# Attention, channel mix and gated convolution in one kernel: new tables for the planner that orders its steps

## The chip, the cores and the metric

The kernel runs on one core of a Trainium2 chip. The time is device time in microseconds (us). TensorE (PE) does the matmuls, VectorE (DVE), ScalarE (ACT) and GpSimd (POOL) the elementwise work; SP issues most of the transfers and POOL those that add to what is there. Every engine works through its own instructions in the order in which the program has them.

## The reference

Three layers follow each other, on 4 batches of 576 tokens of 512 values, in fp32.

```python
# attention: B=4, H=8, S=576, D=64
q_d, k_d, v_d = means of q, k, v over 4 neighbouring tokens
out_up = repeat(softmax(scale * q_d @ k_d.T) @ v_d, 4)
scores = where(abs(i - j) < 4, scale * q @ k.T, -1e9)
x = out_up + softmax(scores) @ v
# channel mix, 512 -> 1024 -> 512
xk = mu_k * x + (1 - mu_k) * x_prev
xr = mu_r * x + (1 - mu_r) * x_prev
k = relu(xk @ w_k)
x = sigmoid(xr @ w_r) * (k * k @ w_v)
# gated convolution, 512 -> 1024 -> 512
h = relu(x @ w_in)
conv_out = convolution of h along the tokens, 3 taps per channel
out = (h * sigmoid(conv_out)) @ w_out
```

## The kernel before

**Attention.** It goes by batch and group of four heads, eight groups in all. The local scores (`local_scores`, L543) put a mask into PSUM with a few bf16 matmuls (L560) and add, block by block of 32 queries, fp32 matmuls with 38 columns each (L569), in two steps of up to 40 instructions. The trace shows two passes for one such fp32 instruction of the program, so 40 instructions are 80 passes. The scores of the pooled keys and queries (`down_scores`, L618) are L634, their softmax's last step, `norm`, is L676 on ACT or L678 on DVE; L707 and L762 transpose probabilities, `down_out` multiplies by the pooled values (L730), and `local_out` by the values (L781, 32 columns, 144 passes a group); L796 adds the two into `xT`. The local matmuls are very short, and there are many of them.

**Channel mix.** fp32 is made of two fp32r parts, high and low, and each product of three matmuls: high by high, low by high, high by low. `mix` (L929) takes half a batch (288 tokens): the up projection is 8 steps of 12 matmuls of 288 columns (L939), the down projection 8 steps of 12 and 12 (L988). The first half of batch 0 is done with exact fp32 weights instead (`first_mix`, L865; L876 and L906). The relu, the square and the splitting of k lie at L958 to L976, on ACT and DVE (the high copy is L969 on ACT or L971 on DVE).

**The rest.** In six chunks of 384 tokens: `gate` (L1260, r), `hidden` (L1301, h, with the convolution on DVE and ACT) and `outp` (L1381, the output).

**Transfers.** `load` (L392) is an SP transfer; `load_sum` (L394) sums four planes of pooled input: one load by SP, and three accumulating ones through POOL's queue (L400), each of which waits for the one ahead. So `kqd` (pooled keys and queries) and `vd` are filled. There is one `kqd` buffer for the groups after the first two, which are split, and an L634 step of 20 instructions (40 passes) reads it; six L634 steps are whole in this way. `vw` holds the values for the local output, `vw_f` and `kq_f` (and `kqd_f`) those of the other group of batch 0. Weights come as 512 KB pieces into one of three `st_d` (L418), and ACT and DVE split them into their parts (L405 to L450). The first matmuls of the program are fill matmuls (L1043), which compute nothing that is used.

**The order.** Each piece of work is a `step` of class `Program` (L83): the engine, an estimated time, a function that emits the instructions, what it reads and writes, and a due time. A step that may go to two engines has two times, and the planner takes the engine. `order` (L126) plays the program through, engine by engine: of the steps that are ready it takes the one that must start earliest. Two tables shift this by the tag of a step, such as `('lo', 2, 0, 0)` for the local output of batch 2, group 0, `('up', b, half)`, `('dn', b, half)` for the projections, or `('wk', 0, column)` for a weight piece:

```python
        latest = [t - EARLY.get(k, 0.0) for t, k in zip(latest, self.tags)]   # L142
        ready = [HOLD.get(k, 0.0) for k in self.tags]                         # L145
            i = min((i for i in q if ready[i] <= at + 1e-9), key=lambda i: (latest[i], i))   # L166
```

HOLD (L25) is the earliest time, in the planner's microseconds, at which a step may stand, EARLY (L38) how much more urgent it is made. What comes out is one list of instructions for each engine.

Of the kernel before, what the change touches and what calls it, by code (L numbers as in the profile page):

```python
# [22 lines left out]


HOLD = {  # L25
    ('dn', 0, 0): 14.9, ('dn', 0, 1): 34.2, ('dn', 1, 0): 21.3, ('dn', 1, 1): 18.4, ('dn', 2, 1): 14.8,
    ('dn', 3, 0): 0.4, ('lc', 2): 18.9, ('lc', 4): 152.4, ('ld', 0, 0, 10): 22.5, ('ld', 0, 1, 0): 8,
    ('ld', 0, 1, 10): 38, ('ld', 2, 0, 0): 11.4, ('ld', 2, 1, 0): 129.6, ('ld', 3, 0, 0): 67.1,
    ('ld', 3, 1, 0): 4.1, ('mu',): 13.5, ('o', 0): 32.1, ('o', 1): 56.9, ('o', 2): 6.4, ('o', 3): 49.8,
    ('o', 5): 44.2, ('sx', 0): 98.7, ('sx', 1): 2.6, ('wi', 0, 0): 2.5, ('wi', 0, 128): 65.5,  # L30
    ('wi', 0, 256): 118.8, ('wi', 0, 384): 49.7, ('wi', 0, 512): 34.8, ('wi', 0, 640): 19.4,
    ('wi', 0, 896): 0.5, ('wk', 0, 0): 20.4, ('wk', 0, 128): 17, ('wk', 0, 256): 5.3, ('wk', 0, 512): 0.5,
    ('wk', 0, 640): 16.4, ('wk', 0, 768): 24.2, ('wk', 0, 896): 0.5, ('wo', 2, 0): 4.2, ('wo', 3, 0): 1.6,
    ('wo', 5, 0): 20.6, ('wo', 6, 0): 26.2, ('wr', 0, 384): 71, ('wv', 0, 0): 4.5, ('wv', 0, 256): 34.3,
    ('wv', 0, 384): 7.3, ('wv', 1, 0): 20.5, ('wv', 1, 128): 31.2, ('wv', 1, 384): 46.9,
}

EARLY = {  # L38
    ('dn', 0, 0): 362.8, ('dn', 0, 1): -820.5, ('dn', 1, 0): -80.4, ('dn', 1, 1): -10.7,
    ('dn', 2, 0): -11.7, ('dn', 2, 1): 29.4, ('dn', 3, 0): 13.7, ('dn', 3, 1): 108.6,  # L40
    ('do', 0, 0, 0): -7.5, ('do', 0, 0, 10): -7.4, ('do', 0, 1, 0): -7.9, ('do', 0, 1, 10): 3,
    ('do', 1, 0, 0): -35.3, ('do', 1, 1, 0): -69.4, ('do', 2, 0, 0): -57.6, ('do', 2, 1, 0): 8.8,
    ('do', 3, 0, 0): 141.6, ('do', 3, 1, 0): 81.4, ('ds', 0, 0, 0): 15.6, ('ds', 0, 0, 10): -410.1,
    ('ds', 0, 1, 0): 4.2, ('ds', 0, 1, 10): 180.9, ('ds', 1, 0, 0): 566, ('ds', 1, 1, 0): 679.3,
    ('ds', 2, 0, 0): 163.7, ('ds', 2, 1, 0): 192.7, ('ds', 3, 0, 0): 300.4, ('ds', 3, 1, 0): -16.4,
    ('fill',): -104.7, ('g', 0): 286.6, ('g', 1): 157.2, ('g', 2): -6.9, ('g', 3): -203.9, ('g', 4): -59.3,
    ('g', 5): 119.1, ('h', 0): 10.9, ('h', 1): -155.2, ('h', 2): -58.5, ('h', 3): -17, ('h', 4): 265.4,
    ('h', 5): 1.6, ('kd', 0, 0, 10): -275.5, ('kd', 0, 1, 0): -135, ('kd', 0, 1, 10): 27.6,
    ('lc', 0): -572.8, ('lc', 1): -205.6, ('lc', 2): 141.2, ('lc', 3): 35, ('lc', 4): -3.8,
    ('lc', 5): 10.4, ('ld', 0, 0, 10): 92.2, ('ld', 0, 1, 0): -2.8, ('ld', 1, 0, 0): 85.9,  # L50
    ('ld', 1, 1, 0): -94.4, ('ld', 2, 0, 0): -275.8, ('ld', 3, 0, 0): -51.1, ('lo', 0, 0, 0): 119.5,
    ('lo', 0, 0, 10): -900.4, ('lo', 0, 1, 0): 61.7, ('lo', 0, 1, 10): 80.1, ('lo', 1, 0, 0): 333,
    ('lo', 2, 0, 0): 355.4, ('lo', 2, 1, 0): 66.8, ('lo', 3, 0, 0): -108.4, ('lo', 3, 1, 0): 586.9,
    ('mp', 0, 0): -756.6, ('mp', 0, 1): -384, ('mp', 1, 0): 197.6, ('mp', 1, 1): -9.5,
    ('mp', 2, 0): -209.6, ('mp', 2, 1): -23.5, ('mp', 3, 0): -20.3, ('mp', 3, 1): -78.3, ('mu',): 73.3,
    ('o', 0): -74, ('o', 1): -220.6, ('o', 2): -203.8, ('o', 3): 416.8, ('o', 5): 6.9,
    ('s', 0, 0, 0): -72.1, ('s', 0, 0, 10): -1335, ('s', 0, 1, 0): -34.3, ('s', 0, 1, 10): -58.1,
    ('s', 1, 0, 0): 382.4, ('s', 1, 1, 0): 29.3, ('s', 2, 0, 0): -39.6, ('s', 2, 1, 0): -999.4,
    ('s', 3, 0, 0): 172.5, ('s', 3, 1, 0): 162.8, ('sx', 0): 90.9, ('sx', 1): -4.2, ('sx', 2): 271.9,
    ('sx', 3): -239.4, ('up', 0, 0): -6.3, ('up', 0, 1): 532, ('up', 1, 0): -0.5, ('up', 1, 1): 94.2,  # L60
    ('up', 2, 0): 589.6, ('up', 2, 1): -2561.6, ('up', 3, 0): 36.8, ('up', 3, 1): -64.9, ('wi', 0, 0): 142,
    ('wi', 0, 128): -81.8, ('wi', 0, 256): -26.9, ('wi', 0, 384): 29.3, ('wi', 0, 512): -117.8,
    ('wi', 0, 640): 2.1, ('wi', 0, 768): -71.3, ('wi', 0, 896): 98, ('wk', 'first'): -1373.2,
    ('wk', 'parts', 0, 0): 39.2, ('wk', 'parts', 0, 128): 105.1, ('wk', 'parts', 0, 256): -391,
    ('wk', 'parts', 0, 384): 158.6, ('wk', 'parts', 0, 512): 67.9, ('wk', 'parts', 0, 640): 32,
    ('wk', 'parts', 0, 768): -824.5, ('wk', 'parts', 0, 896): -168.4, ('wk', 0, 128): -290,
    ('wk', 0, 256): -8, ('wk', 0, 384): 15.7, ('wk', 0, 512): -49.1, ('wk', 0, 640): 166,
    ('wk', 0, 768): 19.3, ('wk', 0, 896): -54.8, ('wo', 0, 0): -27.1, ('wo', 1, 0): 177.6,
    ('wo', 2, 0): 57.8, ('wo', 3, 0): 23.3, ('wo', 4, 0): 188, ('wo', 5, 0): -343.2, ('wo', 6, 0): -6,
    ('wo', 7, 0): 29.1, ('wr', 0, 0): -224.1, ('wr', 0, 128): -173, ('wr', 0, 256): -286.5,  # L70
    ('wr', 0, 384): 265.7, ('wv', 'first'): -29.6, ('wv', 'parts', 0, 0): -23.2,
    ('wv', 'parts', 0, 128): 13.8, ('wv', 'parts', 0, 256): -424.1, ('wv', 'parts', 0, 384): 49,
    ('wv', 'parts', 1, 0): 7, ('wv', 'parts', 1, 128): 3.2, ('wv', 'parts', 1, 256): 13.4,
    ('wv', 'parts', 1, 384): -98.2, ('wv', 0, 0): 8.5, ('wv', 0, 256): -5.3, ('wv', 0, 384): 109.3,
    ('wv', 1, 0): 34.9, ('wv', 1, 128): -120.4, ('wv', 1, 256): 355.1, ('wv', 1, 384): -37.6,
}


# [7 lines left out]
class Program:  # L86
# [19 lines left out]
    def step(self, engine, us, f, r=(), w=(), due=None, slack=1.0):  # L106
        n = len(self.steps)
        deps = set()
        for k in r:
            if k in self.writer:  # L110
                deps.add(self.writer[k])
        for k in w:
            deps.update(self.readers.pop(k, ()))
            if k in self.writer:
                deps.add(self.writer[k])
        for k in r:
            self.readers.setdefault(k, set()).add(n)
        for k in w:
            self.writer[k] = n
        deps.discard(n)  # L120
        self.steps.append((engine, us, f, due, slack))
        self.tags.append(self.tag)
        self.deps.append(deps)
        return n
# [100 lines left out]
def dve(n):  # L225
    return 0.13 + 1.1e-3 * n
# [22 lines left out]
def tile_local_attention__then__channel_mix__then__conv_glu(  # L249
# [24 lines left out]
    SD = S // FAC  # L274
# [70 lines left out]
    first = tc.alloc_tile_pool(name="first", bufs=1)  # L345
# [39 lines left out]
    def ring(name, tiles, one=0):  # L385

        i = count[name] = count.get(name, -1) + 1
        i %= one or len(tiles)
        return tiles[i], (name, i)
# [68 lines left out]
    def group(b, gp):  # L458
# [3 lines left out]
        g = {"kq": ring("kq", kq_t, int(b > 0)), "kqd": ring("kqd", kqd, int(b > 0)), "vw": ring("vw", vw_t, int(b > 0)),  # L462
             "vd": ring("vd", vd_t, int(b > 0))}
# [154 lines left out]
        def down_scores(i0, i1):  # L618
            tag("ds", i0)
            q0, m, qs = down_blocks(i0, i1)  # L620
            nq = len(qs)
            pst, pk = ring("a2", a2_t)
            pd, pdk = ring("pd", pd_t, int(b > 0))
            sm, smk = ring("sums", sums)
# [48 lines left out]
            def norm(eng):  # L673
# [6 lines left out]
                    )  # L680

            step(
                ("DVE", "ACT"), (dve(nq * SD), 0.2 * nq + 0.1), norm, [(smk, "r", r) for r in range(2)],
                [(pdk, r) for r in range(2)], slack=SL[i0 > 0],
            )

# [61 lines left out]
        def local_out(i0, i1):  # L748
# [24 lines left out]
            for pr, hp in enumerate(pairs):  # L773
# [30 lines left out]
                step("DVE", 0.28 + 0.97e-3 * nt, add, [odk], [(pk, 0), (pk, 1)] + ks, slack=SL[i0 > 0])  # L804

        return {"loads": loads, "kqd": pooled_kq, "s": local_scores, "ds": down_scores,
                "do": down_out, "lo": local_out}

# [323 lines left out]
    wo = [t.rearrange("p k c -> p (k c)").rearrange("p (k c) -> p k c", c=DM) for t in wk_t]  # L1132
# [354 lines left out]
```

## Time and profile before

| | before |
|---|---|
| median of 3 runs | 579.89 us (578.99 to 582.29) |
| the profiled execution | 580.39 us |
| its span | 578.7 us |
| mean granted clock of TensorE | 0.991 |
| PE busy | 556.3 us, 96% of the span, 5960 matmul passes |
| DVE busy | 365.4 us, 63% |
| ACT busy | 339.0 us, 59% |
| POOL busy | 47.4 us, 8% |

The profiled execution is 0.50 us above the median of the runs. The share of busy time is a mean over a front part, in which attention, channel mix and all weight loads overlap, and a back part of long matmuls.

### The profile page before, as it was taken

How to read it: one execution, taken by the hardware profiler on the slowest of the kernel's cores; microseconds unless marked ns; L12 is line 12 of the kernel's file. 1: busy time of each engine (PE TensorE's matmuls, PEld its weight loads, DVE VectorE, ACT ScalarE, POOL GpSimd, SP SyncE). 2: the span in 40 equal slices, each digit the busy share in tenths (PEclk: the TensorE clock that was granted, in tenths of full speed). 3: DMA queues.
4: the chain of work that ended last, by engine and by line, in shares of the span. 5: the costliest groups of instructions: out<-in, count | busy, mean ns of one | idle time of the engine just before them, and what ended most of it. 6: DMA issues, size and time to landing. Idle time of an engine off the chain costs nothing.

```text
span 578.7 us, 14428 instructions
## 1 busy us (share of the span) xinstructions
PE 556.3 (96%) x5960; PEld 510.6 (88%) x5960; DVE 365.4 (63%) x749; ACT 339.0 (59%) x810; POOL 47.4 (8%) x150
## 2 busy tenths in 40 slices
PE   7899999969999999799999999999999999999996
PEld 4677789959999899799999989899988998998995
DVE  4898989746344551549307999389747695294580
ACT  3678888638675573559649856356435445263441
POOL 5001111020110202100000000000000000000000
PEclk9989999999999999999999999999999999999999
DMA  8479898991875856608212430401200300100101
GB/s 329 156 222 243 287 295 218 292 327 37 251 209 162 202 161 125 159 2 264 74 42 61 146 109 8 148 11 36 75 38 38 110 1 37 56 1 0 56 1 54
DMA packets 30938, 72.97 MB, mean 126 GB/s; under 512 B 3288, under 2 KB 14040, under 8 KB 29848
## 3 DMA queue, kind: packets, MB, share of 16 engines
q1 hardware_dynamic: 26552, 64.09, 33.3%
q0 software_dynamic: 4320, 7.97, 8.4%
q8 instruction: 46, 0.75, 0.5%
q14 instruction: 20, 0.16, 0.1%
HBM read 57.88 MB, written 14.16 MB: 124 GB/s over the span
## 4 chain that ended last, share of the span: by engine, by line
PE 87%; DVE 4%; issue 3%; ACT 2%; DMA 2%; POOL 1%; ACTq 0%; POOLq 0%; DVEq 0%
PE a L1381 17%; PE mm L939 16%; PE mm L988 14%; PE a L1301 8%; PE mm L1301 7%; PE mm L1260 4%; PE a L1260 4%; PE a L781 3%; PE mm L876 3%; PE mm L906 3%; PE a L730 2%; DMA xT<-x_d 2%; PE a L569 2%; PE a L707 2%; PE a L762 2%
## 5 line engine op out<-in xcount | busy, mean ns | idle before, releaser
L1381 PE MATMUL a<-wk,wv 128*128 128x512 f32 x432 | 100.4, 390 | 0.0
L939 PE MATMUL mm<-xk,wk 128*128 128x288 f32 x672 | 95.7, 302 | 3.3 <-issue 3.3
L939 PEld LDWEIGHTS mm<-xk,wk 128*128 128x128 f32 x672 | 92.5, 194 | 4.2 <-issue 4.0
L988 PE MATMUL mm<-k,wv 128*128 128x288 f32 x672 | 95.9, 298 | 0.1
L1381 PEld LDWEIGHTS a<-wk,wv 128*128 128x128 f32 x432 | 81.0, 188 | 16.2
L988 PEld LDWEIGHTS mm<-k,wv 128*128 128x128 f32 x672 | 90.2, 188 | 1.2 <-ACT k L969 0.2
L976 DVE TENSOR_TENSOR k<-tmp,k 128x288 fp32r<-128x288 f32 x56 | 25.5, 455 | 47.8 <-ACT k L969 47.5
L1301 PE MATMUL mm<-k,wi 128*128 128x386 f32 x288 | 53.0, 338 | 0.7 <-ACT k L1285 0.4
L1301 PE MATMUL a<-k,wi 128*128 128x386 f32 x288 | 52.7, 338 | 0.0
L1301 PEld LDWEIGHTS mm<-k,wi 128*128 128x128 f32 x288 | 50.7, 188 | 1.7 <-ACT k L1285 0.7
L1301 PEld LDWEIGHTS a<-k,wi 128*128 128x128 f32 x288 | 50.8, 188 | 0.2
L1346 DVE TENSOR_SCALAR tmp<-h,cw_sb 128x384 f32<-128x384 f32 x48 | 20.0, 416 | 41.5 <-ACT h L1334 22.2
L1356 ACT ACTIVATE tmp<-tmp 128x384 f32<-128x384 f32 x48 | 25.2, 525 | 27.6 <-DVE tmp L1350 27.5
L958 ACT ACTIVATE tmp<-mm 128x288 f32<-128x288 f32 x56 | 22.9, 409 | 25.4 <-PE mm L939 25.3
L1396 ACT ACTIVATE xT<-a 128x512 f32<-128x512 f32 x18 | 10.3, 595 | 40.3 <-PE a L1381 40.2
L1350 DVE SCALAR_TENSOR_TENSOR tmp<-h,cw_sb,tmp 128x384 f32<-128x384 f32 x48 | 29.7, 619 | 2.6
L1347 DVE SCALAR_TENSOR_TENSOR tmp<-h,cw_sb,tmp 128x384 f32<-128x384 f32 x48 | 29.7, 619 | 2.4
L1368 DVE TENSOR_TENSOR wv<-tmp,wv 128x384 fp32r<-128x384 f32 x48 | 25.5, 553 | 8.9 <-ACT wv L1366 8.6
L1260 PE MATMUL mm<-xk,wr 128*128 128x386 f32 x144 | 26.8, 338 | 0.4 <-ACT h L1329 0.4
L923 ACT COPY tmp<-mm 128x288 f32<-128x288 f32 x32 | 12.5, 395 | 25.0 <-PE mm L988 15.9
L796 DVE TENSOR_TENSOR xT<-a,od 128x288 f32<-128x288 f32 (+2 forms) x40 | 13.8, 392 | 20.6 <-PE a L781 20.3
L400 POOL DMA_DIRECT2D kqd<-in_kqp x18 | 16.0, 889 | 130.4 <-DMA kqd<-in_kqp 81.5
(161 smaller groups left out, 894.5 us busy)
## 6 DMA issues: line engine op xcount, KB each, us to landing
vw<-in_vw SPq DMA_DIRECT2D x7, 1152.0 KB, 8.0
kq<-in_kq SPq DMA_DIRECT2D x6, 1152.0 KB
kqd<-in_kqp POOLq DMA_DIRECT2D x18, 288.0 KB, 7.4
v_d<-tmp SPq DMA_DIRECT2D x32, 144.0 KB, 4.1
x_d<-xT SPq DMA_DIRECT2D x16, 288.0 KB, 4.9
out_dram<-xT SPq DMA_DIRECT2D x18, 256.0 KB, 2.0
st_d<-in_moe_w_k SPq DMA_DIRECT2D x8, 512.0 KB, 5.1
st_d<-in_moe_w_v SPq DMA_DIRECT2D x8, 512.0 KB, 5.2
```

The lines of the kernel that those rows point to most:

```text
L939: nc.tensor.matmul(pst[:, 0:NH], lhsT=wk_t[wt][:, kt, mt * P:(mt + 1) * P], rhs=xk[:, xs, kt, :], start=(kt == 0 and g == 0), stop=(kt == ...
L958: lambda r=r, pst=pst: nc.scalar.activation(r, pst[:, 0:NH], AF.Relu), (), [pk, rk],
L976: ("DVE",), (dve(NH),), lambda e, r=r, kh=kh, kl=kl: e.tensor_sub(kl, r, kh.bitcast(F32)),
L988: nc.tensor.matmul(pst[:, 0:NH], lhsT=wv_t[wt][:, kt, mt * P:(mt + 1) * P], rhs=xs, start=(kt == 0 and g == 0), stop=(kt == KF - 1 and g = ...
L1260: nc.tensor.matmul(pst[:, 0:CW], lhsT=late["wr"][wt][:, kt, mt * P:(mt + 1) * P], rhs=r_t[xs][:, kt, :], start=(kt == 0 and g == 0), stop= ...
L1301: nc.tensor.matmul(pst[:, 0:CW], lhsT=late["wi%d" % (mt * P // HF)][wt][:, kt, mt * P % HF:mt * P % HF + P], rhs=x1s[xs][:, kt, :], start= ...
L1346: nc.vector.tensor_scalar_mul(cv, tap(1), cw[:, 1, mt:mt + 1])
L1347: nc.vector.scalar_tensor_tensor(out=cv, in0=tap(0), scalar=cw[:, 0, mt:mt + 1], in1=cv, op0=ALU.mult, op1=ALU.add)
L1350: nc.vector.scalar_tensor_tensor(out=cv, in0=tap(2), scalar=cw[:, 2, mt:mt + 1], in1=cv, op0=ALU.mult, op1=ALU.add)
L1356: step("ACT", act(CH), lambda: nc.scalar.activation(cv, cv, AF.Tanh, scale=0.5), (), [cvk])
L1368: ("DVE",), (0.56,), lambda e: e.tensor_sub(gl, gf, gh.bitcast(F32)),
L1381: nc.tensor.matmul(pst, lhsT=xs[:, tt * P:(tt + 1) * P], rhs=wo[wt][:, kt, :], start=(kt == 0 and g == 0), stop=(kt == KF - 1 and g == 2),)
```

## The change

The two tables, HOLD and EARLY, have other numbers and partly other entries, and one estimate of the planner is new: `norm` on ACT counts 0.31 us for each of its instructions in place of 0.2. No step is added and none removed.

```diff
 HOLD = {
-    ('dn', 0, 0): 14.9, ('dn', 0, 1): 34.2, ('dn', 1, 0): 21.3, ('dn', 1, 1): 18.4, ('dn', 2, 1): 14.8,
+    ('dn', 0, 0): 61.5, ('dn', 0, 1): 4.9, ('dn', 1, 0): 3.7, ('dn', 2, 0): 9.7, ('dn', 2, 1): 79.5,
...
 EARLY = {
-    ('dn', 0, 0): 362.8, ('dn', 0, 1): -820.5, ('dn', 1, 0): -80.4, ('dn', 1, 1): -10.7,
+    ('dn', 1, 0): -21.5, ('dn', 1, 1): -204.1, ('dn', 2, 0): -1104, ('dn', 2, 1): -77.1,
...
-                ("DVE", "ACT"), (dve(nq * SD), 0.2 * nq + 0.1), norm, [(smk, "r", r) for r in range(2)],
+                ("DVE", "ACT"), (dve(nq * SD), 0.31 * nq + 0.09), norm, [(smk, "r", r) for r in range(2)],
```

Both programs have 4404 matmul instructions on PE. The norm goes to ACT (L676) in three places and to DVE (L678) in seven, before in seven and three; five high copies of k go to DVE instead of ACT. PE's instructions that only wait for an event number 29, before 22. On SP the first loads stood as kq, vw, cw_st, one w_k piece, kq_f, vw_f; now as w_k, kq, w_k, vw, w_k, kq_f, vw_f; 20 fill matmuls stand ahead of the first scores, before 14.

PE, about a fifth into its program: a group's local output (`a_182`, `a_181` are its accumulators in PSUM), the local scores of another group, and the projections around. Before:

```order
L781 MATMUL a_182<-pt_139,vw_133 64x32 x36
L781 MATMUL a_181<-pt_139,vw_133 64x32 x36
L988 MATMUL mm_178<-k_123,wv_117 128x288
...
L560 LDWEIGHTS ident_71
L560 MATMUL a_181<-mask,ident_71 128x38
...
L569 MATMUL a_181<-kq_129 32x38 x72
L939 MATMUL mm_177<-xk_122,wk_115 128x288
L939 MATMUL mm_177<-xk_122,wk_116 128x288
```

Now:

```order
L781 MATMUL a_182<-pt_139,vw_133 64x32 x36
L781 MATMUL a_181<-pt_139,vw_133 64x32 x36
L988 MATMUL mm_178<-k_123,wv_117 128x288
...
L560 LDWEIGHTS ident_71
L560 MATMUL a_181<-mask,ident_71 128x38
...
L569 MATMUL a_181<-kq_129 32x38 x40
L988 MATMUL mm_178<-k_123,wv_117 128x288
L988 MATMUL mm_178<-k_123,wv_118 128x288
...
L939 MATMUL mm_177<-xk_122,wk_115 128x288
```

The two halves of the local scores no longer stand together: 12 matmuls of L988 and then L939 follow the first 40 instructions, and the other 32 come 135 rows later.

PE at the fourth of the six whole L634 steps, which reads `kqd`. Before:

```order
L781 MATMUL a_181<-pt_139,vw_133 64x32 x36
L781 MATMUL a_182<-pt_139,vw_133 64x32 x36
L939 MATMUL mm_178<-xk_121,wk_115 128x288
L939 MATMUL mm_178<-xk_121,wk_116 128x288
...
L634 MATMUL a_181<-kqd_131 32x144 x20
```

Now:

```order
L762 MATMUL a_179<-ident,probs_137 128x128
...
L781 MATMUL a_181<-pt_139,vw_133 64x32 x36
L781 MATMUL a_182<-pt_139,vw_133 64x32 x36
L634 MATMUL a_181<-kqd_131 32x144 x20
L939 MATMUL mm_178<-xk_121,wk_115 128x288
```

The step stood 88 rows behind L781 and now stands right behind it.

PE at the last-but-one local output, with the last whole L634 step. Before:

```order
L781 MATMUL a_181<-pt_139,vw_133 64x32 x36
L781 MATMUL a_182<-pt_139,vw_133 64x32 x36
L634 MATMUL a_181<-kqd_131 32x144 x20
L939 MATMUL mm_177<-xk_121,wk_115 128x288
...
L569 MATMUL a_182<-kq_129 32x38 x40
L939 MATMUL mm_178<-xk_121,wk_115 128x288
...
L569 MATMUL a_182<-kq_129 32x38 x32
```

Now:

```order
L781 MATMUL a_181<-pt_139,vw_133 64x32 x36
L781 MATMUL a_182<-pt_139,vw_133 64x32 x36
L988 MATMUL mm_177<-k_123,wv_117 128x288
...
L634 MATMUL a_181<-kqd_131 32x144 x20
L560 LDWEIGHTS ident_71
...
L569 MATMUL a_182<-kq_129 32x38 x40
L939 MATMUL mm_177<-xk_121,wk_115 128x288
...
L569 MATMUL a_182<-kq_129 32x38 x32
```

12 matmuls of L988 have come between L781 and L634, and the 12 of L939 that stood between L634 and the scores are gone from there.

## Rows read from the trace of the kernel before

**Rows 1.** Busy time by stretch: window, us, PE (x), PEld, DVE, ACT, POOL, clock, DMA share, GB/s.

```profile
260.00:574.00 314.00, 312.89 (x1764) 293.92 (x1762) 205.73 (x403) 167.65 (x372) 7.35 (x70) 1.00 0.19 61
```

**Rows 2.** Waits of PE, 40 to 579 us: line, releaser, total us, times, longest.

```profile
PE a L569 <- issue: 6.2, 3, 3.1
PE mm L939 <- issue: 3.3, 1, 3.3
```

**Rows 3.** Timeline of PE around two waits: start, us, instruction, passes, idle before.

```profile
115.85 2.30 PE L781 MATMUL a<-pt,vw 38*64 38x32 f32 x144
118.08 1.86 PE L988 MATMUL mm<-k,wv 128*128 128x288 f32 x12
119.78 0.49 PE L560 MATMUL a<-mask,ident 128*128 128x38 bf16 x4
120.20 0.34 PE L569 MATMUL a<-kq 64*32 64x38 f32 x25
122.75 1.23 PE L569 MATMUL a<-kq 64*32 64x38 f32 x119 [2.21 <-issue]
123.91 1.46 PE L939 MATMUL mm<-xk,wk 128*128 128x288 f32 x9
128.67 3.66 PE L939 MATMUL mm<-xk,wk 128*128 128x288 f32 x14 [3.31 <-issue]
```

**Rows 4.** The page's busy times and instruction queue; that queue between 120.3 and 121.4 us.

```profile
PE 556.3 (96%) x5960; PEld 510.6 (88%) x5960; DVE 365.4 (63%) x749; ACT 339.0 (59%) x810; POOL 47.4 (8%) x150
...
q8 instruction: 46, 0.75, 0.5%
...
q8 instruction: 1, 0.02, 5.2%
```

**Rows 5.** Timeline of PE at the other two waits, and at a run without one.

```profile
190.54 2.30 PE L781 MATMUL a<-pt,vw 38*64 38x32 f32 x144
...
196.28 0.58 PE L569 MATMUL a<-kq 64*32 64x38 f32 x42 [0.82 <-issue]
...
244.02 0.30 PE L569 MATMUL a<-kq 64*32 64x38 f32 x14 [3.15 <-issue]
...
257.44 2.30 PE L781 MATMUL a<-pt,vw 38*64 38x32 f32 x144
```

**Rows 6.** Timeline of PE, the last whole L634 step.

```profile
234.58 0.96 PE L634 MATMUL a<-kqd 64*32 64x144 f32 x40
```

**Rows 7.** Busy time by stretch, as in rows 1, after the two longest waits.

```profile
128.70:132.10 3.40, 3.40 (x14) 3.40 (x15) 1.85 (x5) 1.39 (x3) 0.86 (x1) 0.50 0.67 137
132.10:135.50 3.40, 3.40 (x28) 3.40 (x27) 2.47 (x7) 2.65 (x7) 0.84 (x1) 0.99 0.19 30
244.80:248.20 3.40, 3.40 (x16) 3.31 (x16) 2.32 (x5) 1.08 (x3) 0.00 (x0) 0.50 0.04 11
```

**Rows 8.** The vw_f load: its issue, its KB and us to landing, its first use.

```profile
3.48 0.47 SPq L392 DMA_DIRECT2D vw_f<-in_vw  x1
...
vw_f<-in_vw SPq DMA_DIRECT2D x1, 1152.0 KB, 12.5
...
19.63 4.48 PE L499 MATMUL mm<-vw_f,tmp 128*72 128x256 f32 x20
```

**Rows 9.** Two chains that fill kqd: SP's load, the last accumulating one, its landing.

```profile
212.26 0.33 SPq L392 DMA_DIRECT2D kqd<-in_kqp  x1
...
226.84 0.87 POOL L400 DMA_DIRECT2D kqd<-in_kqp  x1 [4.16 <-DMA kqd<-in_kqp]
...
kqd<-in_kqp POOLq DMA_DIRECT2D x1, 288.0 KB, 4.9
...
98.56 0.33 SPq L392 DMA_DIRECT2D kqd<-in_kqp  x1
...
123.86 0.89 POOL L400 DMA_DIRECT2D kqd<-in_kqp  x1 [2.37 <-DMA kqd<-in_kqp]
...
kqd<-in_kqp POOLq DMA_DIRECT2D x1, 288.0 KB, 7.5
```

## Prediction before the run

> **What bounds the kernel now.** I read busy time by stretch first. From 260 us to 574 us, where the second half of the kernel runs, TensorE (PE) is busy for 312.89 of 314.00 us [rows 1]: only 1.1 us could be won there without doing less arithmetic, and the change does as many matmuls as before. So an order of steps can gain or lose before 260 us. There I asked what ended each idle stretch of PE. The largest answer is not another engine: it is "issue", time in which nothing that the profile shows was waited for, 6.2 us in three waits ahead of local scores (L569) and 3.3 us in one wait ahead of the up projection (L939) [rows 2]. Together 9.5 us.
>
> The order of events around two of them tells what they are [rows 3]. PE stops in the middle of the local scores, after 25 passes of a step, waits 2.21 us, does 119 passes of L569 and 9 of L939, and stops again for 3.31 us in the middle of an L939 step. 119 + 9 = 128 matmuls. Each goes with a weight load, so 256 instructions lie between the two stops. The queue named "instruction" brought 46 packets, 0.75 MB in all, 16 KB each; 46 times 256 are 11,776, and PE has 5960 matmuls and 5960 weight loads, 11,920. During the 2.21 us one such packet is under way [rows 4]. So I read these waits as PE out of instructions: **a block of 256 was worked off before the packet of the next had come.** The other two waits, 0.82 and 3.15 us, also cut through a run of L569 [rows 5], where a pass of 38 columns is shortest.
>
> What a block takes follows from the same rows. Prices per pass: L781 (118.08 − 115.85)/144 = 0.0155 us; L988 or L939 (119.78 − 118.08)/12 = 0.142; the four mask passes L560 0.42 together; L569 (123.91 − 122.75)/119 = 0.0098 [rows 3]; L634 about 0.96/40, 0.022 to 0.024 [rows 6]. The block that ended in the 2.21 us wait held 87 L781, 12 L988, 4 L560 and 25 L569: from about 116.76 to 120.54, 3.8 us of work, and 6.0 to the next one's start. The one behind it had 2.6 us of work and 5.9 to the next start. The block that ended at 195.46 held 74 L781, 12 L988, 4 L560 and the first 38 of a step of 80 L569: from about 191.6 on, 3.8 us of work and 0.82 of wait, 4.6 [rows 3, 5]. So a following packet was there 4.6 to 6.0 us after a block began. Where a block of short passes lies behind large ones, it isn't late: 144 passes of L781 from 257.44 on ran through without a wait, with L939 ahead of them [rows 5]. Most blocks hold 128 passes of 0.142 us, 18 us, and never wait.
>
> **The change part by part.** It does no work less and none more; the planner's cost for the norm (L683) and the two tables move steps.
>
> *Waits for instructions.* I counted 256 instructions a block through both orders. Before, the four waits give 9.5 us. In the new order the local scores of that place are cut: 80 passes, 12 L988, then L939, and the other 64 passes much later, so that the block of 119 L569 and 9 L939 no longer exists. Short blocks are left. (a) 97 L781, 12 L939, 18 L634: 1.50 + 1.70 + 0.40 = 3.6 us. (b) 78 L781, 12 L988, 4 L560, 34 L569: 1.21 + 1.70 + 0.42 + 0.33 = 3.7. (d) at the last-but-one local scores: 2 L781, 12 L988, 40 L634, 4 L560, 70 L569: 0.03 + 1.70 + 0.88 + 0.42 + 0.69 = 3.7. (f) 22 L634, 22 L939, 4 L560, 80 L569: 0.48 + 3.12 + 0.42 + 0.78 = 4.8. (g) 65 L781, 40 L634, 22 L988: 1.01 + 0.88 + 3.12 = 5.0. Two more are almost all L781 (128 passes, 2.0 us, and 122 with 6 L939, 2.7 us); they follow L988 or L939 like the run at 257.44, and I count nothing. The nearest row for (a), (b) and (d) is the block that ended at 195.46: (b) differs from it by four passes. With its 4.6 us they wait 1.0 + 0.9 + 0.9 = 2.8, (f) and (g) nothing. With the 6.0 us of the busiest place they wait 2.4 + 2.3 + 2.3 + 1.2 + 1.0 = 9.2. With an earlier packet, nothing. I take 2.8, as that row is nearest: **9.5 to 2.8, −6.7 us**, bounds −9.5 and −0.3.
>
> *The clock.* After each of the two waits above 3 us the granted clock stands at 0.50 (1.2 of 2.4 GHz) for 3.4 us, and PE does 14 and 16 matmuls where it does 28 in the next stretch of equal length [rows 7]. Lost: 3.4 × (1 − 14/28) = 1.70 and 3.4 × (1 − 16/28) = 1.46, together 3.2. After the 2.21 us wait PE went on at a full-speed price per pass. None of my remaining waits is above 1.1 us, so **−3.2 us**, bounds −3.2 and 0 (two waits above 3 us left).
>
> *The start.* The loads vw_f and kq_f stand behind two more w_k loads of 512 KB, and more fill matmuls stand ahead of the first scores. vw_f was issued at 3.48, landed 12.5 us later, at 16.0, and was used first at 19.63 [rows 8]: 3.6 us to spare. By 16.0 some 4.6 MB had come (kq, vw, one st_d, kq_f, vw_f), 0.33 MB a us from about 2 us on, so 1.0 MB more is 3.2 us. Just hidden: 0. If its cover is gone (an earlier use), up to +2.5; if the earlier weights release the first mix, −1.
>
> *The pooled keys and queries.* kqd is one buffer, freed by the end of one L634 step and filled for the next by one load from SP and three accumulating loads from POOL, one behind another. In the new order the fourth of the six whole L634 steps stands right behind L781. Between the end of the third and it PE has 108 passes of L988 or L939 (15.3 us), 144 of L781 (2.2), 64 of L569 (0.6), and 35 of L707, L730 and L762, some 2 us: about 20. The chain in the trace took from 212.26 to 226.84 + 4.9, 19.5 us, where no weights were loading, and from 98.56 to 123.86 + 7.5, 32.8 us, where they were [rows 9]. The new order has no weight load on SP behind that kqd load, so I take the 19.5: 0. Bounds 0 and +12.8.
>
> *Other engines.* The norm moves from ACT to DVE in four of ten places, and five copies of k low or high change engine the same way; both engines had room where PE is the bound (205.73 and 167.65 of 314 us busy [rows 1]). Five w_in conversions come later, beyond 260 us. The old order leaves PE 1.1 us of waits there; for new ones I allow **+1.5**, bounds 0 and +4.
>
> *Sum.* The profiled execution took 580.39 us (span 578.7). 580.39 − 6.7 − 3.2 + 1.5 = 572.0. It stood 0.5 above the median of the runs, 579.89, so 571.5 as a median.
>
> **A rule against it.** At four of 46 packets the rows show PE standing still for 0.82 to 3.31 us [rows 2, 3, 5]; at the rest they show nothing. The Trainium skill, page "Runtime: NRT & Kernel Launch", section "Instruction fetch mechanics", says that the sequencer fetches the next 16 KiB block while it executes the current one and that crossing a boundary costs one DMA tail-bump, "mostly hidden". The trace agrees on the size of the block and at most boundaries, and differs at the four. By the rule the term of −6.7 would be nothing, and the time that of rival 2.
>
> **The rivals.**
> 1. *The waits only move.* (a), (b) and (d) meet a full DMA and need the 6.0 us of the busiest place; (f) and (g) then wait too, and the clock falls twice: 571.5 − 2.8 + 9.2 + 3.2 = 581.1. For it: all waits of before lay in the stretch where weights and vw load, and (a) and (b) lie there too. Against it: in the same stretch the block nearest to (b) waited 0.82 us [rows 5], and two of the heavy places follow each other in the old order only. Chance 0.14.
> 2. *The four waits are not for instructions*, but stand with L569 itself, and stay: 580. For it: three of four cut L569. Against it: the 128 passes and the packet. Chance 0.03. The page above is what would lead one to it.
> 3. *Slower: PE waits at the fourth whole L634 for kqd.* The chain takes the 32.8 us instead of 19.5, against 20 us of work: +12.8, and the clock falls once, +1.6: 571.5 + 12.8 + 1.6 = 585.9. It decides when the wait is above some 11 us; half of it leaves the time within 0.5% of before. For it: nothing between the two chains seen is excluded, and one halfway, 26 us, would already make PE wait 6. Against it: what made the chain long were weight loads, which now stand elsewhere. Chance 0.11.
>
> **How the numbers follow.** A measurement of this kernel can tell about 0.5% from no change: the three runs lie between 578.99 and 582.29. That is 577.0 and 582.8. The forecast, 566 to 577, has 0.69 (a single wait of 3 us with its fall of the clock, 576, is in it); rival 1 0.14, of which a fifth lies above 582.8; rival 2 0.03; rival 3 0.11; 0.03 for a start without cover, one third each. Faster: 0.69 + 0.01 = 0.70. Same: 0.11 + 0.03 + 0.01 = 0.15. Slower: 0.03 + 0.11 + 0.01 = 0.15. The range goes down to all waits gone, no new ones and the start's −1: 571.5 − 2.8 − 1.5 − 1 = 566. Upwards it takes in most of rival 1, to 581.5, and leaves out rival 3. The forecast's own range is 566 to 577.
>
> **What would show it.** Right: "issue" ahead of PE falls from 9.5 to 2 to 4 us; a clock of 0.50 after the start is gone; the packets of the instruction queue come while PE works; waits of PE on other engines after 40 us stay under 3 us. Wrong: a wait above 2 us at (a), (b) or (d); an idle stretch ahead of the fourth whole L634 that ends with a kqd transfer; PE below 312 of the last 314 us; a later first L876.

## The result and the profile after

The changed kernel takes 573.18 us as the median of 7 runs (571.11 to 576.04); the kernel before, run beside it, takes 579.89 (578.93 to 582.75). The ratio is 0.988, with a 95% interval of 0.9845 to 0.9914: faster by 1.2%. The forecast was 571.5, faster with a chance of 0.70, so the direction and about the size came as forecast. Taken term by term, the waits, the clock behind them and the other engines came out near what was written; the start, set at nothing, did not.

The profiled execution took 574.89 us, with a span of 573.2 and a clock of 0.988. The waits of PE from 40 us on (line, releaser, total us, times, longest), to be read against [rows 2]:

```profile
PE mm L939 <- issue: 1.1, 2, 0.7
PE a L634 <- DVE xT L796: 0.9, 1, 0.9
PE a L569 <- issue: 0.9, 2, 0.6
PE mm L906 <- DVE st_f L408: 0.9, 1, 0.9
PE a L1381 <- ACT xT L1396: 0.7, 1, 0.7
```

"issue" has gone from 9.5 us in four waits to 2.0 in four, none above 0.75. Three waits on other engines, 2.5 us, are new, where before had 1.0 of such after 40 us.

The timeline of PE at the place of [rows 3], where the second half of the local scores has been moved away:

```profile
122.42 0.49 PE L560 MATMUL a<-mask,ident 128*128 128x38 bf16 x4
122.85 0.47 PE L569 MATMUL a<-kq 64*32 64x38 f32 x34
123.93 0.61 PE L569 MATMUL a<-kq 64*32 64x38 f32 x46 [0.61 <-issue]
124.47 1.85 PE L988 MATMUL mm<-k,wv 128*128 128x288 f32 x12
126.17 5.05 PE L939 MATMUL mm<-xk,wk 128*128 128x288 f32 x37
```

PE stops after 34 passes of L569, just where the count of 256 instructions a block put the end of block (b), and for 0.61 us. After it come 46 passes of L569 and then long ones, and no second stop follows. The other three: the last 10 passes of the last-but-one scores, block (d), 0.27 us; L939 at 202.01, 0.75; L939 at 252.54, 0.34:

```profile
202.01 9.25 PE L939 MATMUL mm<-xk,wk 128*128 128x288 f32 x68 [0.75 <-issue]
...
229.73 0.28 PE L569 MATMUL a<-kq 64*32 64x38 f32 x10 [0.27 <-issue]
...
252.54 0.95 PE L939 MATMUL mm<-xk,wk 128*128 128x288 f32 x6 [0.34 <-issue]
```

Busy time by stretch, in the columns of [rows 1, 7]:

```profile
24.00:28.00 4.00, 3.55 (x119) 3.12 (x119) 3.96 (x11) 2.47 (x8) 0.00 (x0) 0.94 0.57 158
28.00:40.60 12.60, 10.62 (x223) 8.08 (x222) 8.06 (x29) 5.72 (x18) 0.81 (x1) 0.50 0.33 97
44.00:260.00 216.00, 212.18 (x3568) 195.59 (x3568) 134.19 (x282) 147.01 (x369) 30.97 (x43) 1.00 0.72 199
260.00:568.00 308.00, 307.14 (x1726) 288.89 (x1726) 207.18 (x401) 161.48 (x357) 7.20 (x65) 1.00 0.19 62
```

From 44 us on the clock is 1.00 throughout: the two falls of [rows 7] are gone. But from about 27.5 to 41.1 us it stands at 0.50. The kernel before has one such stretch at the start too, of 3.4 us, from about 33.2 on:

```profile
24.00:33.00 9.00, 6.99 (x253) 6.06 (x252) 8.36 (x21) 5.43 (x14) 0.00 (x0) 1.00 0.43 120
33.50:36.90 3.40, 3.40 (x73) 2.59 (x72) 3.30 (x9) 2.62 (x8) 0.15 (x1) 0.55 0.59 146
```

The load of vw_f, which answers to [rows 8], was issued 4.5 us later than before and landed at 8.03 + 10.5 = 18.5, 1.2 us ahead of its use:

```profile
vw_f<-in_vw SPq DMA_DIRECT2D x1, 1152.0 KB, 10.5
...
19.71 4.48 PE L499 MATMUL mm<-vw_f,tmp 128*72 128x256 f32 x20
```

The kqd chain of the fourth whole L634 step, which answers to [rows 9]:

```profile
139.95 0.33 SPq L392 DMA_DIRECT2D kqd<-in_kqp  x1
...
157.49 0.86 POOL L400 DMA_DIRECT2D kqd<-in_kqp  x1 [8.53 <-DMA vd<-in_vp]
...
kqd<-in_kqp POOLq DMA_DIRECT2D x1, 288.0 KB, 4.3
...
161.92 0.96 PE L634 MATMUL a<-kqd 64*32 64x144 f32 x40 [0.90 <-DVE xT L796]
```

It took 157.49 + 4.3 − 139.95 = 21.8 us and landed at 161.79. PE had been ready since 161.02; the wait is put down to L796, which read the accumulator that L634 was to use until 161.90. So kqd came 0.1 us before it would have been the last to arrive.

### The profile page after: what moved, and what is told of

It is laid out like the page before. It is cut to its first block, busy times and chain, and to the rows that moved or that the text cites. A ratio compares the mean times of both kernels' runs of the same rounds, so it can differ in the third digit from the quotient of the medians.

```text
span 573.2 us, 14414 instructions
## 1 busy us (share of the span) xinstructions
PE 555.5 (97%) x5960; PEld 510.4 (89%) x5960; DVE 371.8 (65%) x758; ACT 334.3 (58%) x791; POOL 49.1 (9%) x150
## 4 chain that ended last, share of the span: by engine, by line
PE 91%; DMA 3%; DVE 3%; ACT 1%; issue 1%; ACTq 0%; SPq 0%; DVEq 0%
PE a L1381 17%; PE mm L939 16%; PE mm L988 16%; PE a L1301 9%; PE mm L1301 9%; PE mm L1260 4%; PE a L1260 4%; PE a L781 3%; PE mm L876 3%; PE a L730 2%; PE a L707 2%; PE a L762 2%; PE a L569 2%; DMA kq_f<-in_kq 1%; PE a L634 1%; PE mm L906 1%
## 5 line engine op out<-in xcount | busy, mean ns | idle before, releaser
L1381 PE MATMUL a<-wk,wv 128*128 128x512 f32 x432 | 100.6, 390 | 0.7 <-ACT xT L1396 0.7
L1381 PEld LDWEIGHTS a<-wk,wv 128*128 128x128 f32 x432 | 80.9, 188 | 17.0 <-ACT xT L1396 1.1
L939 PE MATMUL mm<-xk,wk 128*128 128x288 f32 x672 | 94.7, 298 | 1.1 <-issue 1.1
L988 PE MATMUL mm<-k,wv 128*128 128x288 f32 x672 | 95.3, 298 | 0.0
L939 PEld LDWEIGHTS mm<-xk,wk 128*128 128x128 f32 x672 | 90.0, 188 | 2.4 <-issue 1.6
L988 PEld LDWEIGHTS mm<-k,wv 128*128 128x128 f32 x672 | 90.1, 189 | 0.8 <-issue 0.4
L1301 PE MATMUL mm<-k,wi 128*128 128x386 f32 x288 | 53.6, 339 | 0.2
L1301 PE MATMUL a<-k,wi 128*128 128x386 f32 x288 | 53.0, 338 | 0.0
L1301 PEld LDWEIGHTS mm<-k,wi 128*128 128x128 f32 x288 | 50.6, 188 | 1.7 <-DVE k L1287 0.8
L1301 PEld LDWEIGHTS a<-k,wi 128*128 128x128 f32 x288 | 50.8, 188 | 0.2
L1396 ACT ACTIVATE xT<-a 128x512 f32<-128x512 f32 x18 | 10.5, 595 | 48.1 <-PE a L1381 47.7
L958 ACT ACTIVATE tmp<-mm 128x288 f32<-128x288 f32 x56 | 22.9, 410 | 23.7 <-PE mm L939 22.0
L405 DVE SCALAR_TENSOR_TENSOR st_f<-st_f,st_d 128x512 uint32<-128x512 uint32 x28 | 19.2, 687 | 22.2 <-ACT st_d L424 22.2
L796 DVE TENSOR_TENSOR xT<-a,od 128x288 f32<-128x288 f32 (+2 forms) x40 | 13.8, 392 | 21.2 <-PE a L781 13.1
L1359 DVE SCALAR_TENSOR_TENSOR tmp<-tmp,h 128x384 f32<-128x384 f32 x48 | 25.4, 552 | 2.6 <-ACT tmp L1356 2.4
L1366 ACT CAST wv<-tmp 128x384 fp32r<-128x384 f32 x48 | 23.4, 512 | 5.6 <-DVE tmp L1359 5.2
```

Source lines behind the costliest of these rows:

```text
L939: nc.tensor.matmul(pst[:, 0:NH], lhsT=wk_t[wt][:, kt, mt * P:(mt + 1) * P], rhs=xk[:, xs, kt, :], start=(kt == 0 and g == 0), stop=(kt == ...
L988: nc.tensor.matmul(pst[:, 0:NH], lhsT=wv_t[wt][:, kt, mt * P:(mt + 1) * P], rhs=xs, start=(kt == 0 and g == 0), stop=(kt == KF - 1 and g = ...
L1301: nc.tensor.matmul(pst[:, 0:CW], lhsT=late["wi%d" % (mt * P // HF)][wt][:, kt, mt * P % HF:mt * P % HF + P], rhs=x1s[xs][:, kt, :], start= ...
L1359: lambda: nc.vector.scalar_tensor_tensor(out=gt, in0=cv, scalar=1.0, in1=tap(1), op0=ALU.add, op1=ALU.mult),
L1366: step("ACT", act(CH), lambda: nc.scalar.copy(gh, gf), ["wv_old", gk], [("gh", j)])
L1381: nc.tensor.matmul(pst, lhsT=xs[:, tt * P:(tt + 1) * P], rhs=wo[wt][:, kt, :], start=(kt == 0 and g == 0), stop=(kt == KF - 1 and g == 2),)
```

## The experiments

The theory is that PE stands still where a block of 256 instructions holds less work than the next one's packet needs to arrive, and that a packet needs longer the more other transfers are under way. The rivals are that the waits belong to the order of the steps as such (the local scores), or that the arrival time has nothing to do with other traffic. In all ratios, the kernel before ran on the same chip beside the other.

### The same order, other ends of blocks

The strongest test moves no step. The 20 fill matmuls at the start become 84 thin ones, so that each block ends 64 passes earlier in the order:

```diff
-            for _ in range(2):
+            for _ in range([9, 9, 9, 9, 8, 8, 8, 8, 8, 8][k[1]]):
-                    mm_t[1][:, 0:8 * W], lhsT=ident16, rhs=mask[:, 1:2, :].to_broadcast([P, 8, W]),
+                    mm_t[1][:, 0:68], lhsT=ident16, rhs=mask.rearrange("p a w -> p (a w)")[:, 0:68],
```

> The order of the changed kernel, not one step moved; only the 20 fill matmuls at the start become 84 thinner ones of about the same columns in all, so that every block of 256 instructions ends 64 passes earlier in the order. Counted through the order, short blocks then come to lie at more and shorter stretches. If PE's instruction blocks set the waits: the issue waits after 40 us grow from 2.0 to between 5 and 9 us, at other places than in the changed kernel, and the time to about 577 (575 to 581 if the clock falls). If the order of the steps alone sets them, the waits stay at 2.0 us and the time at 573 within 1.5.

Measured: 585.68 us, a ratio of 1.0087 (1.0055 to 1.0119), so 2% above the changed kernel's 0.988. The waits of PE after 40 us:

```profile
PE a L569 <- issue: 7.3, 3, 3.5
PE a L634 <- issue: 2.5, 1, 2.5
PE mm L906 <- issue: 2.4, 1, 2.4
```

"issue" is 12.2 us, more than the 5 to 9 expected, and at places where the changed kernel had none: in the middle of an L906 group with one matmul left, and after 14 of 40 passes of an L634 step:

```profile
71.29 1.97 PE L906 MATMUL mm<-xT,st_ff 128*128 128x288 f32 x7
75.61 0.40 PE L906 MATMUL mm<-xT,st_ff 128*128 128x288 f32 x1 [2.35 <-issue]
...
169.08 0.47 PE L634 MATMUL a<-kqd 64*32 64x144 f32 x14
172.04 1.21 PE L634 MATMUL a<-kqd 64*32 64x144 f32 x26 [2.48 <-issue]
```

The clock stood at 0.50 in four stretches after 44 us, one at each of the four waits above 2 us, for 16.6 us in all. The start isn't what costs: the last 16 matmuls of L876 begin at 57.45 us, in the changed kernel at 58.12. The waits are not tied to the local scores or to the order of the steps: where the blocks end decides.

The number of passes that PE has done at a stop says the same for all kernels. The 13 traces of this study have 45 stops after 40 us that are put down to "issue", and the passes done by then, counted from the program's first and divided by 128, leave a remainder of 82 to 90 at every one (in the kernel before 2009, 2137, 3160 and 3927 passes: 89, 89, 88 and 87). In the shift by 64 it is 83 to 89 as well, though each step of its order has 64 passes more ahead of it. The remainder falls slowly along a program, which fits the few instructions of PE that are neither a matmul nor its weight load.

With 116 thin fill matmuls, 96 passes of shift:

> As the shift by 64, by 96 passes (116 thin fill matmuls for 20). Counted through the order this leaves fewer short blocks than the changed kernel has. If PE's instruction blocks set the waits: issue waits after 40 us of 0.5 to 2.5 us, at other places, and a time of 572 within 2; above all it is faster than the shift by 64 by 2 us or more, though it adds 64 more instructions. If not: no difference between the two.

580.61 us, 0.9997 (0.9971 to 1.0023). Against the shift by 64 it is 5 us faster, though it has 64 more instructions, as expected. Its waits are 5.0 us and not 0.5 to 2.5, and so 572 was missed:

```profile
PE a L569 <- issue: 5.0, 2, 4.4
```

One is 0.60 us, the other, at the last-but-one scores (235.60), 4.42. The count of short blocks was right (two stops for four); the arrival of one packet was not: 8.4 us passed from that block's first pass to the next one's.

### One step moved in the kernel before

```diff
-        for i in self.order():
+        got = self.order()
+        late, at = [525], got.index(473)
+        for i in got[:at + 1]:
+            if i not in late and any(d in late for d in self.deps[i]):
+                late.append(i)
+        late.sort(key=got.index)
+        got = [i for i in got[:at + 1] if i not in late] + late + got[at + 1:]
+        for i in got:
```

Step 525 is the second half of the local scores between the two stops of [rows 3], 473 the fourth L939 step behind it.

> The order of before, with one step moved: the second half of the local scores that stood between the waits of 2.21 and 3.31 us (64 passes of L569), and what depends on it, comes four L939 steps (48 matmuls, 6.4 us) later. If the waits are for PE's instructions, a block of 256, the 2.21 us wait stays, since its block holds the same work, and the 3.31 us wait goes, with its 3.4 us at a clock of 0.50: 3.31 + 1.70 = 5.0 us less than before, about 575. If the waits belong to local scores as such, there are two shorter ones or the same sum, and the time stays within 1 us of before.

It came out slower: 583.91 us, 1.003 (1.0008 to 1.0053). The timeline of PE at that place:

```profile
119.87 0.34 PE L569 MATMUL a<-kq 64*32 64x38 f32 x25
121.23 0.69 PE L569 MATMUL a<-kq 64*32 64x38 f32 x55 [1.02 <-issue]
121.85 6.62 PE L939 MATMUL mm<-xk,wk 128*128 128x288 f32 x48
128.40 0.77 PE L569 MATMUL a<-kq 64*32 64x38 f32 x64
132.14 3.25 PE L939 MATMUL mm<-xk,wk 128*128 128x288 f32 x12 [2.97 <-ACT tmp L958]
135.97 5.03 PE L939 MATMUL mm<-xk,wk 128*128 128x288 f32 x36 [0.58 <-ACT tmp L958]
```

The 3.31 us wait for instructions is gone, as the block theory has it. In its place PE waits 2.97 us for ACT. The scores' softmax was moved with them, and on ACT its exponential (L598) stands ahead of the relus (L958) that free L939's accumulators:

```profile
131.02 0.77 ACT L598 ACTIVATE probs<-probs 128x684 f32<-128x684 f32 x1 [4.33 <-DVE probs L586]
131.70 0.39 ACT L958 ACTIVATE tmp<-mm 128x288 f32<-128x288 f32 x1
```

ACT stood at L598 for 4.33 us with a relu behind it that had nothing to wait for. Waits for instructions of 1.31 us (159.99, where before had none) and 4.18 us (3.15 before) came beside it, and the clock stood at 0.50 for about 13.5 us after 40 us, in the kernel before for about 6.8. So the step in my expectation that failed is "moved with what depends on it": a step cut out of a block must also leave the queues of the other engines in an order that fits.

### Less traffic, the same instructions

In the kernel before, the vw loads of batches 1 to 3 were cut to 256 of 2304 columns. PE's order is word for word that of before.

```diff
-                t.rearrange("p e h d -> p (e h d)"), vw[b, gp], NB // 2 * 4 * D, (), [(k, 0), (k, half)], SL[0],
+                t.rearrange("p e h d -> p (e h d)")[:, 0:256 if b else None], vw[b, gp][:, 0:256 if b else None], NB // 2 * 4 * D, (), [(k, 0), (k, half)], SL[0],
```

> The kernel before, in the same order, with the vw loads of batches 1 to 3 cut from 2304 to 256 columns of a row (1152 to 128 KB); the local output of those batches is computed from what is left in the buffer. PE has the same instructions. If the packet of the next block is late because it queues behind other transfers, then at the place of the 3.15 us wait (240.9), where a vw load was issued 6 us earlier, the wait falls to under 1 us, and the pair near 120 to 128, where a vw load and three others are under way, falls from 5.5 to between 1 and 4 us; with the clock 4 to 8 us in all: 0.987 to 0.993 of the kernel before. If the fetch itself takes 6 us, waits and time stay.

575.53 us, 0.9888 (0.985 to 0.9927). The wait of 3.15 us fell to 0.24 and the stretch at 0.50 behind it went. The pair is still there, 4.55 us for 5.52, which misses the 1 to 4 expected, and around it the clock stood at 0.50 for 10.1 us (124.5 to 134.6):

```profile
122.92 1.23 PE L569 MATMUL a<-kq 64*32 64x38 f32 x119 [2.31 <-issue]
128.57 14.50 PE L939 MATMUL mm<-xk,wk 128*128 128x288 f32 x87 [2.24 <-issue]
241.32 0.30 PE L569 MATMUL a<-kq 64*32 64x38 f32 x14 [0.24 <-issue]
```

At the pair, w_in pieces and two POOL chains fly as well. The next kernel keeps that edit and cuts the w_in and w_out pieces too (L418):

```diff
-        step("SP", dma_us(1024), lambda: nc.sync.dma_start(out=dv, in_=sv), (), [dk])
+        cut_to = 64 if src is w_in or src is w_out else 1024; step("SP", dma_us(1024), lambda: nc.sync.dma_start(out=dv[:, 0:cut_to], in_=sv[:, 0:cut_to]), (), [dk])
```

> The kernel before with the vw loads of batches 1 to 3 cut to 256 of 2304 columns, as in the run on vw alone, and the loads of w_in and w_out pieces cut to 64 of 1024 columns as well; both are computed from what is left in the buffers. PE's instructions stay the same. With vw alone the waits near 122 and 128 us stayed at 2.31 and 2.24. Two w_in pieces (issued near 115 and 122 in the kernel before) fly there too. If the packets of the instruction queue are late because of what other transfers hold the DMA engines, these two waits fall below 1.5 us each, and no wait at the place of 240.9; about 0.980 to 0.988 of the kernel before. If the pair is late for another reason, they stay above 2 us each and the time stays at 0.988.

571.51 us, 0.9806 (0.9764 to 0.9848). The waits of PE after 40 us:

```profile
PE mm L939 <- issue: 1.2, 1, 1.2
PE a L569 <- issue: 0.9, 2, 0.7
```

Of the pair the first wait is gone and the second is 1.20. "issue" is 2.1 us in all, with the order of before and the short blocks that it has, and no clock of 0.50 after 38 us. So both halves of the theory hold: the short block makes the wait possible, and the traffic makes it long. These two kernels move less data and compute something else, so their times hold whatever else lighter traffic gives; the waits are the evidence. A kernel with the weight pieces cut alone wasn't run.

How full the DMA engines are doesn't fix the delay, though. Ahead of the packet that ended the 2.21 us wait of the kernel before, their mean busy share was 1.07 (a packet counts where it starts, so this can pass 1) and the packet started 3.7 us after the block ahead of it began; at the same place with one step moved it was 1.04 and 2.3 us; ahead of the 1.20 us wait here 0.87 and 0.9 us. Which property of the other transfers delays a packet is open.

### The planner's cost and the tables

With the changed tables, the old cost of the norm:

```diff
-                ("DVE", "ACT"), (dve(nq * SD), 0.31 * nq + 0.09), norm, [(smk, "r", r) for r in range(2)],
+                ("DVE", "ACT"), (dve(nq * SD), 0.2 * nq + 0.1), norm, [(smk, "r", r) for r in range(2)],
```

> The changed kernel's tables with the old planner cost of the norm, 0.2 a row plus 0.1: on PE only three L939 steps change places with one local score step. Expected: the changed kernel's time within 1.5 us, so that the tables carry the gain; if the cost carries it, the time of before.

573.96 us, 0.9858 (0.9826 to 0.989); the changed kernel beside it 0.9871 (0.9833 to 0.9908). The tables carry the gain. (In the trace the step that changes places with three L939 steps on PE is one of L707, 2 passes, not of local scores.)

The same two lines the other way round, with the old tables:

> The old tables with the new planner cost of the norm. The plan comes out in another order, and counting blocks of 256 through it gives more short ones than before has: with 4.6 us for the arrival of a packet 6.9 us of waits for 4.1, with 5.2 us 10.7 for 7.7. So issue waits of 11 to 16 us after 40 us where before had 9.5, and 0 to 1.5% slower than before. If the new cost is what helps: faster than before.

593.64 us, 1.0191 (1.0141 to 1.0241): the direction as expected, and more than the 1.5%. The waits of PE after 40 us, the larger ones:

```profile
PE a L569 <- issue: 5.4, 4, 3.6
PE mm L939 <- issue: 4.7, 1, 4.7
PE mm L988 <- issue: 3.1, 2, 2.3
```

"issue" is 13.2 us, within the 11 to 16 expected from the count of short blocks. A plan that changes for another reason moves the blocks' ends as well, and here for the worse.

### The clock at the start

The first kernel adds fill matmuls where PE waits; 42, 50 and 54 are the steps that wait:

```diff
-        for i in self.order():
+        more = {42: 2, 50: 6, 54: 3}
+        for i in self.order():
+            if i in more:
+                self.fill(more[i])
```

> The changed kernel with 11 more fill matmuls (304 columns), put where PE waits between 25 and 33 us: 2 ahead of the L762 step that waits for od, 6 ahead of the L730 step that waits for pdt, 3 ahead of the next L762. If the clock of 0.50 from 27.7 to 40.6 us in the changed kernel comes of PE having little to do there, the clock stays at 1.00 or falls later and for less, and 2 to 4 us come back: about 570. If not, the clock falls as before and the time is 573 to 574.

571.12 us, 0.9839 (0.9809 to 0.9868). Its clock at the start is at 0.50 for some 3 us, from 35 on, instead of 13. But 22 more instructions moved the blocks' ends, and a wait of 1.98 us at 102.23 came in, with 3 us at 0.50 behind it. So the next one adds no instruction:

```diff
+        more = {42: 1, 50: 4, 54: 2}
...
-            for _ in range(2):
+            for _ in range(n or 1 + (k[1] > 6)):
-                    mm_t[1][:, 0:8 * W], lhsT=ident16, rhs=mask[:, 1:2, :].to_broadcast([P, 8, W]),
+                    mm_t[1][:, 0:12 * W], lhsT=ident16, rhs=mask[:, 1:2, :].to_broadcast([P, 12, W]),
```

> The changed kernel with the fill matmuls that are there put elsewhere: 13 of 456 columns at the start for 20 of 304, and 7 of 456 where PE waits between 25 and 33 us (1, 4 and 2). No instruction is added, so the blocks of 256 end where they end in the changed kernel. Expected: issue waits after 40 us of 1.5 to 3 us at the places of the changed kernel, no long stretch at 0.50 before 42 us (under 5 us of it), and 1 to 4 us less than the changed kernel in the same call. If the fills in the waits do nothing for the clock: the time of the changed kernel within 1 us.

570.59 us (569.13 to 572.66), 0.9812 (0.978 to 0.9844), the fastest kernel of the study, and it computes all that the reference asks for. Its waits for instructions after 40 us are 1.3 us, a little under the 1.5 to 3 expected. In its profile the clock is at full speed throughout:

```profile
0.00:28.00 28.00, 22.43 (x397) 14.53 (x398) 20.34 (x43) 17.06 (x44) 9.48 (x41) 1.00 0.76 287
28.00:40.00 12.00, 10.85 (x274) 7.91 (x273) 10.14 (x36) 7.66 (x22) 1.02 (x1) 1.00 0.52 165
40.00:260.00 220.00, 216.22 (x3600) 199.75 (x3600) 134.60 (x281) 146.68 (x368) 31.07 (x43) 1.00 0.72 200
```

The changed kernel ran beside it unedited:

> The changed kernel once more, with nothing edited, beside the others on the same chip. A ratio of 0.988 within 0.004 to the kernel before. If the long stretch at a clock of 0.50 near the start (27.7 to 40.6 us in its first profile) belongs to some executions only, the mean clock of the runs lies between 0.985 and 0.993, and the time goes with it: 571 at 0.993, 575 at 0.986.

573.88 us (571.38 to 578.62), 0.9871. In this profile the clock is at 0.50 from 33 to 39.8 us, half as long as in the first, and once more for 3.4 us from 227.6 on, behind a wait for instructions of 1.38 us; such waits are 2.0 us again, in three places. The seven runs of the result show mean clocks of 0.985 to 0.993. The pairing with the time that I expected isn't a close one: 576.04 at 0.990, 575.28 at 0.985, 571.11 at 0.993. The medians of the two kernels differ by 3.3 us; their intervals against the kernel before overlap by little. Part of what the fills win is lost again: PE waits 2.25 us at L906 for DVE's `st_f` (L408), in the two profiles of the changed kernel 0.88 and 0.67.

> The kernel before with the same fill matmuls put elsewhere as in the best run so far (13 of 456 columns at the start, 7 where PE waits between 25 and 33 us), no instruction added. The kernel before has 3.4 us at a clock of 0.50 near 33.5 us. If the fills hold the clock there too, 1 to 2 us less than before (0.997 of it); the issue waits of 9.5 us and the two later falls of the clock stay. So little would show that the gain of the changed kernel isn't at the start.

580.57 us, 0.9967 (0.9941 to 0.9993): the same fills are worth 0.3% to the old order, and its waits for instructions stay (10.7 us after 40 us). So the 1.2% of the change isn't made at the start; there it loses: the first L876 begins at 34.51 us in the kernel before, at 38.74 in the changed one, at 35.70 with its fills moved.

## Why the prediction was right, and where it wasn't

**Waits for instructions: right.** The term was 9.5 to 2.8, −6.7 us; measured 9.5 to 2.0, −7.5. Blocks (b) and (d) stopped on the very pass that the count gave, for 0.61 and 0.27 us instead of 0.9 each; (a) did not stop; and 1.1 us lie in two blocks that I had set at nothing, since they hold or follow long passes (202.01 and 252.54). At the first the block held some 7 us of work from 194 on, but its packet started only at 199.8. The sum was right, its split only in part, and that makes the closeness of the sum partly luck. What was mis-sized is the arrival, 4.6 to 6.0 us: counted back 128 passes from each stop, the next block's first pass came 4.5 and 4.4 us after (b) and (d) began, 8.1 us at 202.01 and 3.3 at 252.54. The wait of 3.15 us in the kernel before has 6.3 us, so the range was too narrow even for the trace that it was read from. Rival 2, and the rule beside it, are out: one order shows 2.0 or 12.2 us by where its blocks end. The Trainium skill, page "Runtime: NRT & Kernel Launch", section "Instruction fetch mechanics", calls the cost of a boundary "mostly hidden"; the trace agrees where a block is long, and disagrees by up to 4.7 us at one boundary where it is short and other transfers are dense (the old tables with the new cost of the norm).

**The clock after the two long waits: right in this execution.** −3.2 us; no stretch at 0.50 after 42 us. But the reason given, that no wait left is above 1.1 us, didn't hold for every execution: in the second profile one is 1.38 us, and the clock fell behind it. So this term is in part luck.

**Other engines: right.** +1.5 us allowed; 1.0 us before, 2.5 now. L1301 and L1260 no longer wait; L634, L906 and L1381 do.

**The start: the term that failed.** I set it at 0 with bounds −1 and +2.5 and looked only at what the loads could delay. The loads were hidden, as said: vw_f landed at 18.5 where I had 19.2. What was missed is the clock. 580.39 − 7.5 − 3.2 + 1.5 = 571.2, and the profiled execution took 574.89: 3.7 us were lost elsewhere. That is outside my bound of 2.5 (this execution is 1.7 us above the median). The long stretch at 0.50 near the start accounts for most of it: the kernel with the fills moved, whose order on PE is otherwise the same and whose clock doesn't fall, begins its last 16 matmuls of L876 at 53.90 us; the changed kernel, with about 6.8 us at 0.50 in its second profile and 13.6 in its first, at 56.30 and 58.12, 2.4 and 4.2 us later. The kernel before lost some of this too: moving its fills was worth 1.6 us.

The timeline of PE at this place, of the changed kernel in its first and its second profile and of the one with the fills moved:

```profile
58.12 4.05 PE L876 MATMUL mm<-tmp,st_ff 128*128 128x288 f32 x16
```

```profile
56.30 4.05 PE L876 MATMUL mm<-tmp,st_ff 128*128 128x288 f32 x16
```

```profile
53.90 4.05 PE L876 MATMUL mm<-tmp,st_ff 128*128 128x288 f32 x16
```

The trace of before had the warning: 3.4 us at 0.50 from 33.2 on, behind a stretch in which PE was busy for 6.99 of 9.00 us. I had noted the fill matmuls ahead of the first scores and named a later first L876 as a sign of an error (it came 4.2 us later), but had priced neither with the clock. Why the clock falls at 27.5 us in one execution and at 33 in another of the same program is open.

**Rival 1** didn't come: no wait above 0.75 us, 1.38 in the second profile. The shift by 64 shows what it would have cost: about 2%.

**Rival 3** came near. The kqd chain took 21.8 us against 19.5 taken and 32.8 feared, and landed 0.1 us before another wait ended; in the shift by 96 L634 waited 0.17 us for kqd. It wasn't weights that lengthened it: SP issued none in that time. The profile puts the wait ahead of its last part, 8.53 us, down to a vd load that SP issued at 154.52, which I had not counted; in the second profile it puts the wait there, 6.83 us, down to the part of kqd ahead. So what lengthened it is open.

## What to carry to other kernels

Where an engine's idle time is put down to "issue", count its instructions between two stops; if they are a fixed number, look for blocks of short instructions, and put long ones between them, or see which large transfers are under way when the next block is asked for (here they were cut to show it; moving them wasn't tried). A change of the instruction count anywhere ahead (even of fill instructions) moves every later boundary and cost 2% here in one case and 1% in another, so compare two orders with their boundaries counted, and read the waits of each version rather than its time alone. Fill matmuls may do more in the waits where PE would otherwise idle than ahead of the first work: moving seven of 20 there was worth 3.3 us in the changed kernel and 1.6 us in the one before.

## What was not expected of the hardware

A packet of 16 KB of instructions, one of 46 with 0.75 MB in all [rows 4], is held up by the data's transfers: with other traffic cut, waits of 3.15 and 2.21 us became 0.24 and nothing with the same instructions. And a fall of the clock needs no wait above 3 us, as I had it: behind 1.98 us of wait it stood at 0.50 for 3 us, and behind 1.38 us in the unedited kernel's second profile too; behind 2.31 us with the vw loads cut it did so for 10 us; behind 1.10 us in the fastest kernel it did not fall, nor behind the 2.21 us of the kernel before until the next stop. Busy time behind the 1.38 us:

```profile
228.00:231.00 3.00, 3.00 (x74) 2.64 (x73) 0.08 (x1) 0.88 (x3) 0.00 (x0) 0.50 0.97 304
```
